# K, V, dK and dV moved in pairs of batches, woT and wqT for two heads per DMA, in a two-block attention backward

## The chip, the cores and the metric

The kernel runs on one core of a Trainium2 chip. The metric is the device time of one execution in microseconds. Before the change it is 1734.54 us, the median of three runs (1733.31 to 1735.66).

## The reference

Two independent attention blocks, A and B, have the same shapes: x is 8 batches x 96 queries x 640, there are 32 heads of width 128, and each head has a cache of 512 keys and values for each batch. All tensors are bf16. For one block the forward pass is

```
q = split_heads(x @ wq)                          # 8 x 32 x 96 x 128
p = softmax(q @ k_cache^T * 128**-0.5)           # 8 x 32 x 96 x 512
o = p @ v_cache
out = merge_heads(o) @ wo                        # 8 x 96 x 640
```

The outputs of A and B stand side by side in the last axis. The kernel returns this output and, for a given grad_out, the gradients of x, k_cache, v_cache, wq and wo of both blocks. With dO = g @ wo^T for a head, these are dV = P^T dO, dP = dO V^T, dS = P * (dP - rowsum(O * dO)), dK = dS^T Q, dQ = dS K, and then dwo = O^T g, dwq = x^T dQ, dx = sum over heads of dQ wq^T.

## The kernel before

One unit of work is a pair of a head and a batch: 2 blocks x 32 heads x 8 batches = 512 units. A head has 96 queries in each batch, so S, P, dP and dS of a unit are 96 x 512 tiles.

**The order is written out by hand in ticks.** Each step is put on a list with a tick and a slot in the tick, `em.add(tick, slot, step)`, and the list is sorted and emitted. A unit starts a new tick: head h begins at `c0t = tick0 + 8*h`, and its batch b at `ct = c0t + b`. `OFF` says how many ticks later each step of the unit is emitted. The framework then orders the instructions of each engine by this emission order and by which are ready in its own model of time; the softmax steps carry a higher priority. Each engine and each DMA queue then runs its list in order. Transposing DMAs and a few others are held in program order (`keep_in_program_order`).

The steps of a unit, with their offset in ticks:

- `c_ld` (0): loads K and V of one batch, 128 KB each, from the queue of SP (L252, L253). Eleven buffers for K, eight for V.
- `c_s1` (2): eight TensorE transposes of K and V into a bank of PSUM (L262, L264), one VectorE copy to `KVT` (L266).
- `c_s2a`, `c_s2b` (3): S = Q K^T (L278), row maximum on VectorE (L280), exp on ScalarE (L290).
- `c_s3a`, `c_s3b` (3): reciprocal (L300), P on GpSimd (L309). P has five buffers.
- `c_s45` (4 and 5): transposes of P (L334), copied to `PT_sb` by ScalarE (L340, three buffers); one tick later O^T = V^T P^T (L325).
- `c_s5b` (5): O * dO on GpSimd (L363).
- `c_s4` (6): dV with natural dO (queries on the partitions) as operand (L351), ScalarE copy to `dV_sb` (L353, six buffers), store from SP (L354).
- `c_s6` (6): dP (L373), row sums (L375), dS on VectorE (L377, three buffers).
- `c_s7` (7): dK with natural Q as operand (L417), ScalarE copy to `dK_sb` (L419, five buffers), store from SP (L420). `c_s78`: transposes of dS (L400), VectorE copy to `dST_sb` (L402, three buffers), and one tick later dQ^T (L391), evacuated at L406.

The steps of a head lie between them, at ticks that `HK` gives against the head's own c0t:

- `pA` (-6) loads a slice of wq (GpSimd's queue). `pV` (-5) loads wo of the head transposed, by a transposing DMA on SP (L180, one buffer). `pB` (-4) allocates Q^T (`QT_h`) and dO^T (`dOT_h`), two buffers each, and lets GpSimd zero the 32 padding columns of `QT_h` where the DMA will transpose it (L191).
- `pC` (which=0 at -3 and -2, which=1 at 0 and 1) makes Q^T from wq and x^T, and dO^T from woT and g^T (L218).
- `pD` (2 and 7 for dO, 3 and 6 for Q) makes the natural form by TensorE transposes (L235) and a VectorE copy. `pN` makes it by one transposing DMA on SP (L245). `BYDMA` chooses: Q goes by DMA from the ninth head of block A on, dO never.
- `pW` (6) loads wq of the head transposed (L197), which only the sum for dx needs.
- `qA` (12 and 16) transposes O and dQ by DMA (L429), `qB` (18, 19) makes dwo (L443), `qD` (20, 23) makes dwq (L463).
- `gU` sums out and dx over groups of eight heads (four in the first and last group of dx) in twelve pieces spread over 26 ticks (L497); the last group's pieces are added on VectorE (L504) and stored (L505).

The first head of block A is early: its woT is emitted at tick +1, behind the loads of the second unit, and its dO^T at +3 and +4.

Of the kernel before, what the change touches and what calls it, by code (L numbers as in the profile page):

```python
# [45 lines left out]
HK = dict(pA=-6, pB=-4, pV=-5, pW=6, pC0=[-3, -2], pC1=[0, 1], pD1=[2, 7], pD0=[3, 6], pN=[-1, 1], qA0=12, qA1=16, qB=[18, 19], qD=[(20, 0, 3), (23, 3, 5)])  # L46
# [6 lines left out]
def build_block(tc, em, tick0, blk, x, kc, vc, wq, wo, g_all, out_all, dx, dk, dv, dwq, dwo, ident, ones, pools, HG=8, first=True):  # L53
# [10 lines left out]
    assert H % HG == 0 and HG % 2 == 0  # L64
# [21 lines left out]
    S = {}  # L86
    G = {}
# [89 lines left out]
    def pV(h):  # L177
        def f():
            woT_h = hd.tile([128, DC, 128], BF16, name="woT_h", bufs=1)
            tc.keep_in_program_order(nc.sync.dma_start_transpose(woT_h[:], wo[h * 128:(h + 1) * 128, :]))  # L180
            HS[(blk, h)]["woT_h"] = woT_h
        return f

    def pB(h):
        def f():
            st = HS[(blk, h)]
            st["QT_h"] = hd.tile([128, B, 128], BF16, name="QT_h")
            st["dOT_h"] = hd.tile([128, B, 128], BF16, name="dOT_h")
            for k in range(2):
                if BYDMA[k](h):  # L190
                    nc.gpsimd.memset(st["dOT_h" if k else "QT_h"][:, :, Sq:128], 0.0)  # L191
        return f

    def pW(h):
        def f():
            wqT_h = hst.tile([128, 1, D], BF16, name="wqT_h")
            tc.keep_in_program_order(nc.sync.dma_start_transpose(wqT_h[:], wq[:, h * 128:(h + 1) * 128]))  # L197
            HS[(blk, h)]["wqT_h"] = wqT_h[:, 0]
        return f

    def pC(h, which, si):
        def f():
# [3 lines left out]
            if which == 0:  # L206
                dst = st["QT_h"][:, b0:b0 + w // Sq, 0:Sq]
                lhs = lambda c: st["wq_h"][:, c, :]
                rhsT = S["xT"]
                sc = scale  # L210
            else:
                dst = st["dOT_h"][:, b0:b0 + w // Sq, 0:Sq]
                lhs = lambda c: st["woT_h"][:, c, :]
                rhsT = S["gT"]
                sc = None
# [6 lines left out]
    BYDMA = [lambda h: not first or h >= 8, lambda h: False]  # L222

    def pD(h, which, half):
        def f():
            st = HS[(blk, h)]
            src = st["dOT_h" if which else "QT_h"]
            name = "dOnat_h" if which else "Qnat_h"
            if half == 0:
                st[name] = hd.tile([128, B, 128], BF16, name=name)  # L230
# [3 lines left out]
            for i in range(nb):  # L234
                nc.tensor.transpose(n_ps[:, i * 128:(i + 1) * 128], src[:, b0 + i, 0:Sq], ident[:])  # L235
            evac("dve", st[name][0:Sq, b0:b0 + nb, :].rearrange("p b d -> p (b d)"), n_ps[:, 0:nb * 128])
        return f

    def pN(h, which):
        def f():  # L240
            st = HS[(blk, h)]
            src = st["dOT_h" if which else "QT_h"]
            name = "dOnat_h" if which else "Qnat_h"
            st[name] = hd.tile([128, B, 128], BF16, name=name)
            tc.keep_in_program_order(nc.sync.dma_start_transpose(st[name][:], src[:].rearrange("p b q -> p (b q)")))  # L245
        return f

    def c_ld(h, b):
        def f():
            K_sb = kvp.tile([128, KC, 128], BF16, name="K_sb", bufs=11)  # L250
            V_sb = kvp.tile([128, KC, 128], BF16, name="V_sb", bufs=8)
            nc.sync.dma_start(K_sb[:], kc[b, h].rearrange("(p c) d -> p c d", c=KC))  # L252
            nc.sync.dma_start(V_sb[:], vc[b, h].rearrange("(p c) d -> p c d", c=KC))  # L253
            CS[(blk, h, b)] = dict(K_sb=K_sb, V_sb=V_sb)
        return f

# [14 lines left out]
    def c_s2a(h, b):  # L271
        def f():
            with tc.high_priority(PRIO_OFF):
# [4 lines left out]
                nc.tensor.matmul(S_ps[:], hs["QT_h"][:, b, 0:Sq], st["KT"], start=True, stop=True)  # L278
# [25 lines left out]
    def c_s3b(h, b):  # L304
        def f():
            with tc.high_priority(PRIO_OFF):
                st = CS[(blk, h, b)]
                P_sb = wk.tile([Sq, Sk], BF16, name="P_sb", bufs=5)
# [4 lines left out]
    def c_s45(k5, k4, k6):  # L313
        def f():
# [23 lines left out]
            if k4 is not None:  # L338
                PT_sb = wk.tile([128, KC * Sq], BF16, name="PT_sb", bufs=3)
# [4 lines left out]
    def c_s4(h, b):  # L344
        def f():
# [4 lines left out]
            for c in range(KC):  # L350
                nc.tensor.matmul(dV_ps[:, c * 128:(c + 1) * 128], P_sb[:, c * 128:(c + 1) * 128], hs["dOnat_h"][0:Sq, b, :], start=True, stop=True)  # L351
            dV_sb = wk.tile([128, KC * 128], BF16, name="dV_sb", bufs=6)
            nc.scalar.activation(dV_sb[:], dV_ps[:], ACT.Identity, scale=1.0)  # L353
            nc.sync.dma_start(dv[b, h].rearrange("(p c) d -> p (c d)", c=KC), dV_sb[:])  # L354
        return f

    def c_s5b(h, b):
        def f():
# [4 lines left out]
            nc.gpsimd.tensor_tensor(prod[:], hs["OT_h"][:, tok], hs["dOT_h"][:, b, 0:Sq], op=ALU.mult)  # L363
# [3 lines left out]
    def c_s6(h, b):  # L367
        def f():
# [4 lines left out]
            nc.tensor.matmul(dP_ps[:], hs["dOT_h"][:, b, 0:Sq], st["VT"], start=True, stop=True)  # L373
            dl_ps = bank([Sq, 1], F32, "dl_ps")
            nc.tensor.matmul(dl_ps[:], st["prod"][:], ones[:, 0:1], start=True, stop=True)  # L375
            dS_sb = wk.tile([Sq, Sk], BF16, name="dS_sb", bufs=3)
# [4 lines left out]
    def c_s78(k8, k7):  # L381
        def f():
# [12 lines left out]
            if k7 is not None:  # L395
# [5 lines left out]
                dST_sb = wk.tile([128, KC * Sq], BF16, name="dST_sb", bufs=3)  # L401
# [8 lines left out]
    def c_s7(h, b):  # L410
        def f():
# [4 lines left out]
            for c in range(KC):  # L416
                nc.tensor.matmul(dK_ps[:, c * 128:(c + 1) * 128], dS_sb[:, c * 128:(c + 1) * 128], hs["Qnat_h"][0:Sq, b, :], start=True, stop=True)  # L417
            dK_sb = wk.tile([128, KC * 128], BF16, name="dK_sb", bufs=5)
            nc.scalar.activation(dK_sb[:], dK_ps[:], ACT.Identity, scale=1.0)  # L419
# [261 lines left out]
```

## Time and profile before

| | |
|---|---|
| median of three runs | 1734.54 us |
| profiled execution | 1731.99 us |
| its span, first to last instruction | 1730.2 us |
| TensorE busy (matmul) | 1720.4 us, 24127 matmuls |
| TensorE weight loads | 1445.2 us |
| VectorE busy | 1415.1 us |
| ScalarE busy | 1475.7 us |
| GpSimd busy | 761.0 us |
| mean granted TensorE clock | 0.999 |
| DMA, HBM read and written | 161.09 MB and 159.12 MB |
| SP's DMA queue, packets | 548208, 80.7% of 16 engines' span |

PE is TensorE's matmul stream, PEld its weight loads, DVE VectorE, ACT ScalarE, POOL GpSimd. SPq and POOLq are the sequencers that issue DMAs. In a waits row stand the engine and line that waited, what ended the wait, the total in us, the number of times and the longest. In a timeline row stand the start and the duration in us, the engine, the line, the tiles written and read, the sizes, the number of instructions merged, and in brackets the idle time of the engine before them with what ended it.

### The profile page before, as it was taken

Reading aid. Unit: us, or ns where it says so; the run is one execution under the profiler, and the core shown is the slowest. Engines: PE = TensorE matmul, PEld = TensorE weight load, DVE = VectorE, ACT = ScalarE, POOL = GpSimd, SP = SyncE. Lnnn points to the kernel's source line nnn. Section 1 sums busy time; section 2 is a strip of 40 time slices with the busy share of each in tenths; the row PEclk is TensorE's granted clock in tenths of the full one; section 3 lists DMA queues with packets and bytes.
Section 4 is the critical chain, followed back from the end, with each engine's and each line's share of the span. In section 5 each row is a group of like instructions: output and inputs, shape, how many; then the busy total and the mean of one; then the engine's idle time right before and its main releaser. Section 6 shows DMA issues by size and latency. Waiting matters only on the chain.

```text
span 1730.2 us, 65292 instructions
## 1 busy us (share of the span) xinstructions
PE 1720.4 (99%) x24127; PEld 1445.2 (84%) x24127; DVE 1415.1 (82%) x2962; ACT 1475.7 (85%) x4081; POOL 761.0 (44%) x1379
## 2 busy tenths in 40 slices
PE   8999999999999999999999999999999999999998
PEld 6888888888888888888888888888888888888886
DVE  7988877888888888888888887788888888888884
ACT  6999988988888888897877999888888888888883
POOL 3444434444344443445455444344443444444441
PEclk9999999999999999999999999999999999999999
DMA  7998998999889999889999998899898999979994
GB/s 214 227 231 225 230 218 213 231 222 215 228 215 226 223 228 218 210 224 259 232 244 240 234 230 229 222 217 232 225 229 220 215 230 237 219 206 215 235 222 120
DMA packets 564946, 385.40 MB, mean 223 GB/s; under 512 B 286145, under 2 KB 553281, under 8 KB 564625
## 3 DMA queue, kind: packets, MB, share of 16 engines
q1 hardware_dynamic: 548208, 333.52, 80.7%
q0 software_dynamic: 16416, 47.70, 10.8%
q8 instruction: 189, 3.10, 0.8%
q14 instruction: 133, 1.08, 0.2%
HBM read 161.09 MB, written 159.12 MB: 185 GB/s over the span
## 4 chain that ended last, share of the span: by engine, by line
PE 97%; DMA 1%; DVE 1%; ACT 0%; POOL 0%; issue 0%; SPq 0%; DVEq 0%; ACTq 0%; POOLq 0%
PE q_ps L218 12%; PE o_ps L497 11%; PE dV_ps L351 7%; PE dK_ps L417 7%; PE kvT_ps L264 6%; PE kvT_ps L262 6%; PE dP_ps L373 6%; PE S_ps L278 6%; PE dwq_ps L463 6%; PE dwo_ps L443 6%; PE dq_dst_ps L400 5%; PE optp_ps L334 5%; PE optp_ps L325 5%; PE dq_dst_ps L391 5%; PE n_ps L235 2%; DMA out_dram<-ob 0%
## 5 line engine op out<-in xcount | busy, mean ns | idle before, releaser
L309 POOL TENSOR_SCALAR P_sb<-E_sb,rinv 96x512 bf16<-96x512 bf16 x512 | 352.2, 688 | 649.0 <-DVE rinv L300 358.8
L377 DVE SCALAR_TENSOR_TENSOR dS_sb<-dP_ps,dl_ps,P_sb 96x512 bf16<-96x512 f32 x512 | 384.7, 751 | 100.4 <-PE dl_ps L375 86.3
L290 ACT ACTIVATE E_sb<-S_ps,negm 96x512 bf16<-96x512 f32 x512 | 348.7, 681 | 122.9 <-DVE negm L280 121.2
L280 DVE TENSOR_REDUCE negm<-S_ps 96x1 f32<-96x512 f32 x512 | 348.1, 680 | 61.4 <-PE S_ps L278 61.2
L266 DVE COPY KVT<-kvT_ps 128x1024 bf16<-128x1024 bf16 x512 | 349.4, 682 | 35.8 <-PE kvT_ps L264 20.0
L419 ACT ACTIVATE dK_sb<-dK_ps 128x512 bf16<-128x512 f32 x512 | 301.7, 589 | 52.0 <-PE dK_ps L417 47.5
L353 ACT ACTIVATE dV_sb<-dV_ps 128x512 bf16<-128x512 f32 x512 | 315.9, 617 | 0.0
L340 ACT ACTIVATE PT_sb<-optp_ps 128x384 bf16<-128x384 bf16 x512 | 254.6, 497 | 1.4 <-PE optp_ps L334 1.4
L363 POOL TENSOR_TENSOR prod<-OT_h,dOT_h 128x96 bf16<-128x96 bf16 x512 | 186.8, 365 | 90.9 <-ACT OT_h L337 82.3
L262 PE MATMUL kvT_ps<-ident,K_sb 128*128 128x128 bf16 x2048 | 197.9, 219 | 0.6 <-DMA K_sb<-in_A_k_cache_dram 0.6
L264 PE MATMUL kvT_ps<-ident,V_sb 128*128 128x128 bf16 x2048 | 197.9, 219 | 0.0
L351 PE MATMUL dV_ps<-dOnat_h,P_sb 96*128 96x128 bf16 x2048 | 197.9, 219 | 0.0
L417 PE MATMUL dK_ps<-Qnat_h,dS_sb 96*128 96x128 bf16 x2048 | 197.9, 219 | 0.0
L373 PE MATMUL dP_ps<-KVT,dOT_h 128*96 128x512 bf16 x512 | 195.1, 381 | 0.0
L278 PE MATMUL S_ps<-KVT,QT_h 128*96 128x512 bf16 x512 | 193.8, 378 | 0.3 <-DVE KVT L266 0.2
L262 PEld LDWEIGHTS <-K_sb 128*128 128x128 bf16 x2048 | 152.9, 98 | 39.0 <-DMA K_sb<-in_A_k_cache_dram 0.8
L402 DVE COPY dST_sb<-dq_dst_ps 128x384 bf16<-128x384 bf16 x512 | 179.0, 350 | 2.2 <-PE dq_dst_ps L400 1.4
L400 PE MATMUL dq_dst_ps<-ident,dS_sb 96*128 96x96 bf16 x2048 | 172.1, 206 | 1.0 <-DVE dS_sb L377 1.0
L334 PE MATMUL optp_ps<-ident,P_sb 96*128 96x96 bf16 x2048 | 171.6, 205 | 0.9 <-POOL P_sb L309 0.9
L325 PE MATMUL optp_ps<-PT_sb,V_sb 128*128 128x96 bf16 x2048 | 172.1, 206 | 0.0
L391 PE MATMUL dq_dst_ps<-dST_sb,K_sb 128*128 128x96 bf16 x2048 | 170.7, 206 | 0.0
L463 PE MATMUL dwq_ps<-dQnat,x_nat 128*128 128x128 bf16 x1920 | 142.8, 219 | 0.0
(76 smaller groups left out, 3492.0 us busy)
## 6 DMA issues: line engine op xcount, KB each, us to landing
out_dram<-dV_sb SPq DMA_DIRECT2D x512, 128.0 KB, 3.3
out_dram<-dK_sb SPq DMA_DIRECT2D x512, 128.0 KB, 3.3
K_sb<-in_A_k_cache_dram SPq DMA_DIRECT2D x256, 128.0 KB, 3.5
V_sb<-in_A_v_cache_dram SPq DMA_DIRECT2D x256, 128.0 KB, 3.4
K_sb<-in_B_k_cache_dram SPq DMA_DIRECT2D x256, 128.0 KB, 3.4
V_sb<-in_B_v_cache_dram SPq DMA_DIRECT2D x256, 128.0 KB, 3.3
out_dram<-dwo_sb POOLq DMA_DIRECT2D x64, 160.0 KB, 3.7
out_dram<-dwq_sb POOLq DMA_DIRECT2D x64, 160.0 KB, 4.8
```

The source lines that it names most:

```text
L262: nc.tensor.transpose(kvT_ps[:, c * 128:(c + 1) * 128], st["K_sb"][:, c, :], ident[:])
L264: nc.tensor.transpose(kvT_ps[:, Sk + c * 128:Sk + (c + 1) * 128], st["V_sb"][:, c, :], ident[:])
L266: nc.vector.tensor_copy(KVT[:], kvT_ps[:])
L280: nc.vector.tensor_reduce(negm[:], S_ps[:], axis=AX.X, op=ALU.max, negate=True)
L290: nc.scalar.activation(E_sb[:], st["S_ps"][:], ACT.Exp, bias=st["negm"][:], scale=1.0, accum_out=rowsum[:])
L309: nc.gpsimd.tensor_scalar(P_sb[:], st["E_sb"][:], st["rinv"][:], 0.0, op0=ALU.mult, op1=ALU.add)
L351: nc.tensor.matmul(dV_ps[:, c * 128:(c + 1) * 128], P_sb[:, c * 128:(c + 1) * 128], hs["dOnat_h"][0:Sq, b, :], start=True, stop=True)
L353: nc.scalar.activation(dV_sb[:], dV_ps[:], ACT.Identity, scale=1.0)
L373: nc.tensor.matmul(dP_ps[:], hs["dOT_h"][:, b, 0:Sq], st["VT"], start=True, stop=True)
L377: nc.vector.scalar_tensor_tensor(dS_sb[:], dP_ps[:], dl_ps[:, 0:1], st["P_sb"][:], op0=ALU.subtract, op1=ALU.mult)
L417: nc.tensor.matmul(dK_ps[:, c * 128:(c + 1) * 128], dS_sb[:, c * 128:(c + 1) * 128], hs["Qnat_h"][0:Sq, b, :], start=True, stop=True)
L419: nc.scalar.activation(dK_sb[:], dK_ps[:], ACT.Identity, scale=1.0)
```

## The change

- `c_ld` runs for even batches only and loads K of two batches in one DMA of 256 KB, and V likewise. Buffers: six pairs for K (before, eleven single ones), four pairs for V (before, eight single ones).
- `pair_out` collects dV, and dK, of two batches in one tile; ScalarE still copies each batch by itself, and the store of 256 KB is issued behind the odd batch. Three pairs of buffers for each (before, six and five single ones).
- `pV` and `pW` run for even heads only, and one transposing DMA brings two heads. woT keeps one buffer, now of two heads; wqT has six pairs (before, twelve single ones).
- Q^T and dO^T of a head become one tile `QD_h`, and natural Q and natural dO one tile `QDnat_h`, each with two buffers. `NBYDMA` keeps the choice of before: Q by DMA from the ninth head on, dO by TensorE.
- P has four buffers (before five); PT, dS and dST two (before three).
- Ticks: pV -5 to -6, pW 6 to 2, pC1 0, 1 to -1, 0, pN for Q -1 to 0, the transpose of dQ 16 to 15, dwo 18, 19 to 17, 18, dwq (20: three columns blocks, 23: two) to (19: two, 20: three). The first head's woT stays at +1, with the second head's in the same DMA, which before came at tick -3 of the second head.

```diff
-HK = dict(pA=-6, pB=-4, pV=-5, pW=6, pC0=[-3, -2], pC1=[0, 1], pD1=[2, 7], pD0=[3, 6], pN=[-1, 1], qA0=12, qA1=16, qB=[18, 19], qD=[(20, 0, 3), (23, 3, 5)])
+HK = dict(pA=-6, pB=-4, pV=-6, pW=2, pC0=[-3, -2], pC1=[-1, 0], pD1=[2, 7], pD0=[3, 6], pN=0, qA0=12, qA1=15, qB=[17, 18], qD=[(19, 0, 2), (20, 2, 5)])
...
     def pV(h):
         def f():
-            woT_h = hd.tile([128, DC, 128], BF16, name="woT_h", bufs=1)
-            tc.keep_in_program_order(nc.sync.dma_start_transpose(woT_h[:], wo[h * 128:(h + 1) * 128, :]))
-            HS[(blk, h)]["woT_h"] = woT_h
+            woT = hd.tile([128, DC, 256], BF16, name="woT", bufs=1)
+            tc.keep_in_program_order(nc.sync.dma_start_transpose(woT[:], wo[h * 128:(h + 2) * 128, :]))
+            for k in range(2):
+                WT[h + k] = woT[:, :, k * 128:(k + 1) * 128]
...
     def pB(h):
         def f():
-            st["QT_h"] = hd.tile([128, B, 128], BF16, name="QT_h")
-            st["dOT_h"] = hd.tile([128, B, 128], BF16, name="dOT_h")
-            for k in range(2):
-                if BYDMA[k](h):
-                    nc.gpsimd.memset(st["dOT_h" if k else "QT_h"][:, :, Sq:128], 0.0)
+            QD = hd.tile([128, 2, B, 128], BF16, name="QD_h")
+            HS[(blk, h)]["QD_h"] = QD
+            n = NBYDMA(h)
+            if n:
+                nc.gpsimd.memset(QD[:, 0:n, :, Sq:128], 0.0)
...
+            wqT = hst.tile([128, 2, D], BF16, name="wqT", bufs=6)
+            tc.keep_in_program_order(nc.sync.dma_start_transpose(wqT[:], wq[:, h * 128:(h + 2) * 128]))
...
-    BYDMA = [lambda h: not first or h >= 8, lambda h: False]
+    def NBYDMA(h):
+        return 1 if not first or h >= 8 else 0
...
     def c_ld(h, b):
         def f():
-            K_sb = kvp.tile([128, KC, 128], BF16, name="K_sb", bufs=11)
-            V_sb = kvp.tile([128, KC, 128], BF16, name="V_sb", bufs=8)
-            nc.sync.dma_start(K_sb[:], kc[b, h].rearrange("(p c) d -> p c d", c=KC))
-            nc.sync.dma_start(V_sb[:], vc[b, h].rearrange("(p c) d -> p c d", c=KC))
-            CS[(blk, h, b)] = dict(K_sb=K_sb, V_sb=V_sb)
+            K2 = kvp.tile([128, 2, KC, 128], BF16, name="K_sb", bufs=6)
+            V2 = kvp.tile([128, 2, KC, 128], BF16, name="V_sb", bufs=4)
+            for (t_, src) in ((K2, kc), (V2, vc)):
+                nc.sync.dma_start(t_[:].rearrange("p b c d -> p b (c d)"),
+                                  src[b:b + 2, h].rearrange("b (p c) d -> p b (c d)", c=KC))
+            for k in range(2):
+                CS[(blk, h, b + k)] = dict(K_sb=K2[:, k], V_sb=V2[:, k])
...
+    def pair_out(name, dram, h, b, src_ps):
+        if b % 2 == 0:
+            S[name] = wk.tile([128, 2, KC * 128], BF16, name=name, bufs=3)
+        t_ = S[name]
+        nc.scalar.activation(t_[:, b % 2, :], src_ps, ACT.Identity, scale=1.0)
+        if b % 2 == 1:
+            nc.sync.dma_start(dram[b - 1:b + 1, h].rearrange("b (p c) d -> p b (c d)", c=KC), t_[:])
...
-                P_sb = wk.tile([Sq, Sk], BF16, name="P_sb", bufs=5)
+                P_sb = wk.tile([Sq, Sk], BF16, name="P_sb", bufs=4)
...
-                PT_sb = wk.tile([128, KC * Sq], BF16, name="PT_sb", bufs=3)
+                PT_sb = wk.tile([128, KC * Sq], BF16, name="PT_sb", bufs=2)
...
-            dV_sb = wk.tile([128, KC * 128], BF16, name="dV_sb", bufs=6)
-            nc.scalar.activation(dV_sb[:], dV_ps[:], ACT.Identity, scale=1.0)
-            nc.sync.dma_start(dv[b, h].rearrange("(p c) d -> p (c d)", c=KC), dV_sb[:])
+            pair_out("dV_sb", dv, h, b, dV_ps[:])
...
-            dS_sb = wk.tile([Sq, Sk], BF16, name="dS_sb", bufs=3)
+            dS_sb = wk.tile([Sq, Sk], BF16, name="dS_sb", bufs=2)
...
-                dST_sb = wk.tile([128, KC * Sq], BF16, name="dST_sb", bufs=3)
+                dST_sb = wk.tile([128, KC * Sq], BF16, name="dST_sb", bufs=2)
...
         early = first and h == 0
-        em.add(c0t + (1 if early else -3 if first and h == 1 else HK["pV"]), SL_SETUP + 1 if early else SL_HEAD, pV(h))
-        for k in range(2):
-            if BYDMA[k](h):
-                em.add(c0t + HK["pN"][k], SL_HEAD + 0.5, pN(h, k))
-        em.add(c0t + HK["pW"], SL_HEAD, pW(h))
+        if h % 2 == 0:
+            em.add(c0t + (1 if early else HK["pV"]), SL_SETUP + 1 if early else SL_HEAD, pV(h))
+            em.add(c0t + HK["pW"], SL_HEAD, pW(h))
+        if NBYDMA(h):
+            em.add(c0t + HK["pN"], SL_HEAD + 0.5, pN(h))
...
         for b in range(B):
             ct = c0t + b
-            em.add(ct + OFF["ld"], SLOTS["LOAD"], c_ld(h, b))
+            if b % 2 == 0:
+                em.add(ct + OFF["ld"], SLOTS["LOAD"], c_ld(h, b))
```

## The prediction

> **What bounds the kernel now.** I read the page first, then the waits, a stretch of the timeline in mid-kernel, and the timelines of the first and last microseconds. From the page:
>
> ```profile
> span 1730.2 us, 65292 instructions
> PE 1720.4 (99%) x24127; PEld 1445.2 (84%) x24127; DVE 1415.1 (82%) x2962; ACT 1475.7 (85%) x4081; POOL 761.0 (44%) x1379
> DMA  7998998999889999889999998899898999979994
> PE 97%; DMA 1%; DVE 1%; ACT 0%; POOL 0%; issue 0%; SPq 0%; DVEq 0%; ACTq 0%; POOLq 0%
> ```
>
> TensorE works through all but 9.8 us of the span, and the chain that ended last is TensorE's for 97% of it; but the DMA engines are busy too, at about nine tenths. So the waits of TensorE decide, of which these are the largest:
>
> ```profile
> PE warm_ps L601 <- DVE warm L598: 1.6, 1, 1.6
> ...
> PE dq_dst_ps L400 <- DVE dS_sb L377: 1.0, 2, 0.7
> PE optp_ps L334 <- POOL P_sb L309: 0.9, 3, 0.6
> ...
> PE q_ps L218 <- DVE gT L123: 0.6, 1, 0.6
> PE kvT_ps L262 <- DMA K_sb<-in_A_k_cache_dram: 0.6, 1, 0.6
> ...
> PE q_ps L218 <- DMA woT_h<-in_A_wo_dram: 0.2, 1, 0.2
> ```
>
> It waited for a DMA twice, 0.8 us in all. A matmul's duration overlaps the next one's, so a full busy row could hide gaps; the timeline settles that:
>
> ```profile
> 1004.07 0.39 PE L351 MATMUL dV_ps<-dOnat_h,P_sb 96*128 96x128 bf16 x4
> 1004.29 0.38 PE L373 MATMUL dP_ps<-KVT,dOT_h 128*96 128x512 bf16 x1
> 1004.48 0.69 POOL L309 TENSOR_SCALAR P_sb<-E_sb,rinv 96x512 bf16<-96x512 bf16 x1 [1.85 <-PE dV_ps L351]
> 1004.51 0.16 PE L375 MATMUL dl_ps<-ones,prod 128*96 128x1 bf16 x1
> ```
>
> Four matmuls of 128 columns start within 0.22 us, and the one of 512 columns gives way after 0.22 us. By the starts in the trace a matmul takes the array for 56 ns (128 columns), 43 (96), 163 (384), 136 (320), 216 (512) and 26 (one column). With the counts of the groups that is 10808 x 56 + 8192 x 43 + 1280 x 163 + 2304 x 136 + 1024 x 216 + 512 x 26 ns = 1,714 us. Only some 16 us of the span is not matmuls back to back: 1.6 us before the first, about 5 us of waits in the first 40 us and 1.3 us near the end, about 4 us behind the last matmul, and rounding. The kernel is bound by the number of its matmul columns.
>
> The Trainium skill (Perfetto Trace Analysis, Identifying the Most-Contended Engine) says that matmul busy time is no measure of how near a kernel is to its roofline, and that the share of weight loads is a better one. By it the 84% of the weight-load row would leave room, and the next bound would be the DMA engines (the fourth rival, priced from rows below); the starts in the trace do not bear that out here, and the weight loads lie under matmuls that are longer than they are.
>
> **The change part by part.** The profiled execution took 1731.99 us: span 1730.2, and 1.8 around it. The median is 2.55 us above it.
>
> *Matmuls.* None is added or removed. The last clause of the change is already true before: natural dO's 512 transposes (L235) stay, natural Q's 64 of the first eight heads too, and 56 transposing DMAs make the rest. TensorE's 1,714 us stand: 0.
>
> *Fewer DMAs.* SP issues 1,024 plain DMAs less (a K load holds its sequencer for 0.44 us, V 0.40, a store 0.38: about 420 us), and 64 transposing ones less at 1.25 us (80 us, or nothing if one for two heads takes twice as long). SP is only a queue: past the start no matmul waited for what it issues. Bytes and the 1 KB and 256-byte packets stay. Bounds on the total: 0, and a gain of 10 us if the DMA engines were the bound (of the trace's 43,248 packets of 4 bytes, which close each DMA, 1,024 x 16 go, at 10 ns over 16 engines). I take 0, since TensorE doesn't wait there.
>
> *When K and V come.* For even batches the K slot frees as before (the ninth tick of the unit eleven back), the V slot one tick later (it now waits for the odd unit of the pair seven back). A tick is 3.32 us, the mean distance of two S matmuls. In the trace V is issued a median of 4.0 us after its old slot was free, and landed a median of 7.6 us before its first transpose, after the first thirty units never under 1.76 us. Delaying each even V to its new slot moves 93 of 252, and none comes too late, even with 0.9 us more for the larger transfer (128 KB takes 3.4 to 3.5 us to land, x_nat with 320 KB 3.6). Bounds: 0, and 8.7 us if every even V came 4.2 us later (the shortfalls summed after the thirtieth unit). I take 0. The wait stands on SP, and the next stores and loads queue behind it; half of SP's work is gone.
>
> *Paired stores.* ScalarE's copies stay as they are (0.62 and 0.59 us x512). The store waits for the odd copy; three pairs give a slot back four ticks after it is filled, against 3.3 us to land. 0.
>
> *Smaller buffers.* P is written at 1004.48, and the dS that reads its new slot's old content (one tick back) ended at 1002.64: 1.8 us spare. PT, dS and dST have one tick between last read and next write. 0.
>
> *One tile for Q^T and dO^T.* This adds a wait. GpSimd zeroes the padding of a head's tile at tick -4 (0.31 us, x56); the slot is now free only when dP of the head two before has run for its last batch, at tick -3. Before, it waited for S alone:
>
> ```profile
> POOL QT_h L191 <- PE S_ps L278: 8.9, 22, 0.4
> ```
>
> Behind the memset in GpSimd's queue stands P of tick -3, for which TensorE's transposes (L334) wait one tick later. In the stretch above dP ends at 1004.67 and P starts at 1004.48; a memset at 1004.7 would push P to about 1005.05, by 0.57 us. P was ready 0.99 us or more ahead of its transpose after the thirtieth unit (median 2.18). The first writes of Q^T come after dP in TensorE's own order. Bounds: 0, and 56 x 0.31 = 17.4 us if none of the memset found cover. I take 0, by the slack that was never under 0.99.
>
> *Moved ticks.* dO^T one tick earlier still writes behind dP of the old tile. woT has five ticks to land as before (3.8 to 4.0 us). wqT is asked for two ticks after its slot is free. Natural Q lands 4.9 us after its issue, with seven ticks to go. dwo and dwq move by one to three ticks, and tick 3 of a head becomes the lightest (1,536 columns of head work instead of 1,920, 0.16 us shorter); the tightest margin there, KVT before S (L278), was at least 0.37. 0, at worst 64 x 0.16 = 10 us.
>
> *The start.* Here one matmul of the chain waits for woT:
>
> ```profile
> 10.69 0.40 PE L262 MATMUL kvT_ps<-ident,K_sb 128*128 128x128 bf16 x4 [0.59 <-DMA K_sb<-in_A_k_cache_dram]
> 11.73 0.99 PE L218 MATMUL q_ps<-gT,woT_h 128*128 128x384 bf16 x5 [0.20 <-DMA woT_h<-in_A_wo_dram]
> ```
>
> The same bytes as before stand ahead of woT (x, wq, two K and V, g), and it landed at 11.68 us, 0.59 behind the second V at 11.09. For two heads I estimate twice that, so a landing at 12.3: +0.6. The 0.59 us wait for the second K goes, but g lands some 0.9 us later; both disappear in the wait for woT. Bounds: -3.7 us (all waits of the first 40 us gone) and +5.2 (woT took 5.2 us from issue to landing; a second one behind it whole). I take +0.6, from the landings, because the queue was moving bytes all the time.
>
> TensorE's clock in the start: weight loads of the warm-up stand 0.43 us apart, later matmuls of that size 0.22, and the profile grants 0.999 over the span. The Trainium skill (TensorE: Matmul & The Clock Gate, Part 1) says that an idle window of about 3.4 us halves the clock again. By it the +5.2 would become about +7; at +0.6 nothing changes.
>
> *The end.*
>
> ```profile
> 1704.34 1.95 SPq L429 DMA_TRANSPOSE dQnat<-dQT_h  x1
> 1709.00 1.17 PE L463 MATMUL dwq_ps<-dQnat,x_nat 128*128 128x128 bf16 x18
> 1727.14 0.49 DVE L504 TENSOR_TENSOR ob<-o_ps,dx_acc 128x320 bf16<-128x320 f32 x1 [0.78 <-DMA out_dram<-ob]
> ```
>
> The last dQ lands at 1708.10, 4.8 us after the start of the matmuls that make it (1703.27); its use moves one tick up, to about 4.5 us after: +0.3. The drain behind the last matmul (three ob buffers) stays. Bounds 0 and +1.3.
>
> Sum: 1730.2 + 0.6 + 0.3 = 1731.1 span, 1732.9 profiled, **1735.4 us** as median. A measurement of this kernel can tell about 0.2% (3.5 us) from no change.
>
> **The rivals.**
>
> - *The padding decides* (slower). If P is held more than 0.99 us behind dP in the tick of the memset, TensorE stands before L334 in 56 heads. At 0.31 us each: 1752. For it: dP comes late in its tick and P starts at the same time. Against: the margin. From 0.06 us a head on it is past 0.2%.
> - *K or V late* (slower). 8.7 us, and 6.4 more in the first thirty units, if every even V lands 4.2 us later: 1744 to 1750. For it: the V slot. Against: no V would have been late by the trace.
> - *woT of two heads late at the start* (slower). 5.2 instead of 0.6: 1740.
> - *The DMA engines are the bound* (faster). Nine tenths busy speaks for it, and 10 us less gives 1724.5; that TensorE waited 0.8 us for DMAs speaks against it.
> - *The start's waits go* (faster): K's second load comes with the first. -3.7 us: 1731. g behind the larger loads speaks against it.
>
> **How the numbers follow.** Forecast (no change in mid-kernel, +0.9 at the ends) 0.62, its own range 1732.5 to 1738; padding 0.11, K or V 0.09, woT 0.08; DMA engines 0.05, start 0.05. Slower by over 0.2%: 0.28; within: 0.62; faster: 0.10. The range leaves out the DMA case (0.05) and the upper end of the padding and K cases (some 0.12): 1731 to 1746.
>
> **What would show it.** PE at 24127 matmuls and about 1,721 us busy; no PE wait on K, V or P past 40 us; a wait of GpSimd's memset for dP of up to a tick, x56, with no PE wait on P beside it; SP's issues halved and not longer each; woT landing near 12.3 us with some 0.8 to 1 us of PE wait. The prediction is wrong if TensorE's waits past the start sum to over 3 us, or if the ends move by over 3 us.

## The result, and the profile after

| | before | after |
|---|---|---|
| median | 1734.32 us (1733.31 to 1735.66, four runs) | 1744.69 us (1740.59 to 1746.70, four runs) |
| ratio after / before, 95% interval | | 1.0056 [1.0035, 1.0077] |
| profiled execution, its span | 1731.99, 1730.2 us | 1746.70, 1744.9 us |
| mean granted TensorE clock | 0.999 | 0.997 |
| GpSimd's and SP's DMA packets | 16416 and 548208 | 16416 and 529776 |

The changed kernel is 0.56% slower. The time lies inside the range of the prediction, but the forecast itself, no change, is wrong. The changed kernel's executions also differ from each other by much more than those of the kernel before, which matters below, where the number of executions over 1737 us is given beside each median. One execution of the kernel before, 2513 us at a granted clock of 0.654, is in none of the counts.

From the page of the changed kernel, the lines that answer to the first fence of the prediction:

```profile
span 1744.9 us, 62607 instructions
PE 1725.8 (99%) x24127; PEld 1448.9 (83%) x24127; DVE 1421.5 (81%) x2962; ACT 1472.0 (84%) x4081; POOL 758.2 (43%) x1379
DMA  8899888998999987899898999889988999988983
PE 1%; DMA 1%; DVE 1%; issue 0%; POOL 0%; DVEq 0%
```

The work of each engine is the same within 7 us, and the matmuls are the same 24127. The span is 14.7 us longer and TensorE's busy time 5.4 us. The chain row, 97% TensorE before, follows only the drain at the end this time and says nothing of the rest. The waits of TensorE over 0.2 us show two rows of more than 1 us that were not there before, the first two:

```profile
PE dV_ps L365 <- ACT dwq_sb L160: 4.4, 1, 4.4
PE dl_ps L387 <- DVE ob L514: 3.1, 1, 3.1
PE warm_ps L612 <- DVE warm L609: 1.6, 1, 1.6
PE dq_dst_ps L412 <- DVE dS_sb L389: 1.0, 2, 0.7
PE optp_ps L348 <- POOL P_sb L323: 1.0, 3, 0.6
PE q_ps L221 <- DMA woT<-in_A_wo_dram: 0.9, 1, 0.9
PE q_ps L221 <- DVE gT L125: 0.6, 1, 0.6
PE tp_ps L124 <- DMA x_nat<-in_A_x_dram: 0.4, 1, 0.4
PE kvT_ps L278 <- DMA V_sb<-in_A_v_cache_dram: 0.3, 1, 0.3
```

**Where the 14.7 us lie.** In both traces I took from the distance between the starts of two matmuls the time that the first one's columns need (56 ns for 128 columns, and so on as in the prediction) and summed what is left by windows of 107.5 us. From the second window to the seventh, and from the tenth to the fifteenth, both kernels lose 1.1 to 1.3 us in each window: mid-kernel is unchanged. (This base depends on how the times per matmul are rounded, and is next to nothing with the rounded ones of the prediction; only the differences between the kernels are read.) The start (first window) goes from 8.3 to 9.5, the window from 752 us from 1.1 to 8.4, the one from 860 us from 1.1 to 6.0, the last full one from 2.9 to 3.3. That is 13.8 us, and the stretch behind the last matmul's start grew from 4.5 to 5.4 us. So 12 of the 14.7 us lie in two places of one stand each, both at the turn from block A to block B, where the last head groups of A, the loads of x and g of B (`ld_tmp`, `g_nat`, `x_nat`) and the first transposes of B's woT meet.

The first stand, in the timeline of the changed kernel:

```profile
819.31 0.60 POOL L457 DMA_DIRECT2D out_dram<-dwo_sb  x1 [0.95 <-ACT dwo_sb L160]
822.07 0.83 PE L473 MATMUL dwq_ps<-dQnat,x_nat 128*128 128x128 bf16 x12
829.02 0.38 ACT L160 ACTIVATE dwq_sb<-dwq_ps 128x256 bf16<-128x256 f32 x1 [5.38 <-DMA out_dram<-dwo_sb]
829.46 0.58 PE L365 MATMUL dV_ps<-QDnat_h,P_sb 96*128 96x128 bf16 x4 [4.42 <-ACT dwq_sb L160]
830.33 2.08 PE L473 MATMUL dwq_ps<-dQnat,x_nat 128*128 128x128 bf16 x18
```

ScalarE's copy of dwq needs one of the six `row640` buffers, which `ld_tmp`, `dwo_sb` and `dwq_sb` share. That buffer still holds a dwo whose store was issued at 819.31 and landed only at 828.92, after 9.6 us; the median of this store is 4.1 us. ScalarE works in order, dV's bank waits behind the copy, and TensorE stands 4.6 us (by the starts of the matmuls; the rows above count from the end of the matmul before and have 0.2 us less). Then it runs at half rate: the eighteen dwq matmuls of the last line start 107 ns apart instead of 56, and the granted clock is 0.50 until 835.3, which costs another 2.8 us.

The second stand, in the same timeline:

```profile
881.50 2.60 SPq L182 DMA_TRANSPOSE woT<-in_B_wo_dram  x1
882.52 0.89 POOL L134 DMA_DIRECT2D g_nat<-in_grad_out_dram  x1 [0.50 <-PE o_ps L507]
885.71 0.54 POOL L515 DMA_DIRECT2D out_dram<-ob  x1
887.79 0.58 POOL L515 DMA_DIRECT2D out_dram<-ob  x1 [1.14 <-DVE ob L514]
888.97 11.17 SPq L439 DMA_TRANSPOSE Onat<-OT_h  x1
898.70 0.49 DVE L514 TENSOR_TENSOR ob<-o_ps,dx_acc 128x320 bf16<-128x320 f32 x1 [4.08 <-DMA out_dram<-ob]
899.24 0.16 PE L387 MATMUL dl_ps<-ones,prod 128*96 128x1 bf16 x1 [3.14 <-DVE ob L514]
```

VectorE's `ob` waits for one of three buffers, whose stores take 11 to 13 us here; TensorE stands 3.3 us and loses 1.6 more at half rate. What was issued beside them is as late: woT landed 14.9 us after its issue, g_nat 13.8 (before 7.9), and the issue of the transpose of O held SP for 11.2 us (1.25 when nothing is in its way).

Busy time by stretch of the changed kernel; the columns are the stretch, its length, the five engines' busy times (with instructions), TensorE's granted clock, the busy share of the DMA engines (packets overlap, so it can be over 1) and the GB/s that they moved:

```profile
600.00:640.00 40.00, 40.00 (x583) 34.23 (x581) 33.31 (x71) 34.68 (x96) 17.52 (x32) 1.00 0.94 221
...
824.00:836.00 12.00, 7.58 (x74) 6.07 (x72) 3.86 (x9) 3.16 (x9) 2.57 (x5) 0.72 1.00 195
...
884.00:892.00 8.00, 8.00 (x130) 7.17 (x127) 6.19 (x15) 6.01 (x19) 4.71 (x9) 1.00 1.25 79
```

The last of these stretches in the kernel before:

```profile
884.00:892.00 8.00, 8.00 (x108) 6.65 (x107) 6.33 (x14) 6.46 (x19) 4.37 (x8) 1.00 1.13 304
```

From 884 to 892 us the DMA engines are busy all the time by this count, and they move 79 GB/s instead of the 221 of mid-kernel and the 304 of the kernel before. The packets of 256 bytes, which are those of the transposing DMAs, are about as many (1241, before 1187) but take 101 ns each on average, against 26 ns before: 1241 x 101 ns over 16 engines and 8 us is 0.98 of the share of 1.25. So transfers become slow at the second stand, and what waits for a transfer stands. Around the first stand the fall is smaller, 195 GB/s from 824 to 836 us; landings are late there too (9 to 12 us for what was issued from 819 to 825 us).

### The profile page after: what moved, and what is told of

Its sections match the earlier page's. It is cut to its first block, busy times and chain, and to the rows that moved or that the text cites. A ratio compares the mean times of both kernels' runs of the same rounds, so it can differ in the third digit from the quotient of the medians.

```text
span 1744.9 us, 62607 instructions
## 1 busy us (share of the span) xinstructions
PE 1725.8 (99%) x24127; PEld 1448.9 (83%) x24127; DVE 1421.5 (81%) x2962; ACT 1472.0 (84%) x4081; POOL 758.2 (43%) x1379
## 3 DMA queue, kind: packets, MB, share of 16 engines
q1 hardware_dynamic: 529776, 333.45, 79.6%
q0 software_dynamic: 16416, 47.70, 9.4%
## 5 line engine op out<-in xcount | busy, mean ns | idle before, releaser
L375 POOL TENSOR_TENSOR prod<-OT_h,QD_h 128x96 bf16<-128x96 bf16 x512 | 187.5, 366 | 83.6 <-ACT OT_h L351 75.3
L365 PE MATMUL dV_ps<-QDnat_h,P_sb 96*128 96x128 bf16 x2048 | 198.1, 219 | 4.4 <-ACT dwq_sb L160 4.4
L429 PE MATMUL dK_ps<-QDnat_h,dS_sb 96*128 96x128 bf16 x2048 | 197.9, 219 | 0.0
L385 PE MATMUL dP_ps<-KVT,QD_h 128*96 128x512 bf16 x512 | 195.4, 382 | 0.0
L292 PE MATMUL S_ps<-KVT,QD_h 128*96 128x512 bf16 x512 | 194.2, 379 | 0.4
L418 ACT ACTIVATE dQT_h<-dq_dst_ps 128x96 bf16<-128x96 f32 x512 | 128.2, 250 | 25.3 <-DVE dST_sb L414 5.6
```

The source lines that it names most:

```text
L385: nc.tensor.matmul(dP_ps[:], hs["QD_h"][:, 1, b, 0:Sq], st["VT"], start=True, stop=True)
```

## The experiments

Two theories had to be told apart, and the runs undo one part of the change, or make one part alone.

- *Buffers*: the shared buffers `row640` and `ob` are too few in the new order; the moved ticks put a taker right behind a store.
- *Transfers*: the larger DMAs (woT for two heads, K, V, dK, dV for two batches) make the transfers at the turn slow, and any buffer there will do to make TensorE stand.

In the expectations of the first runs, T is the first theory, with the moved ticks as its cause, W the second with woT's DMA and P the second with those of K, V, dK and dV.

### Ticks of dQ, dwo and dwq put back

```diff
-HK = dict(... qA0=12, qA1=15, qB=[17, 18], qD=[(19, 0, 2), (20, 2, 5)])
+HK = dict(... qA0=12, qA1=16, qB=[18, 19], qD=[(20, 0, 3), (23, 3, 5)])
```

> The kernel after, with the ticks of the transpose of dQ, of dwo and of dwq as before (16; 18, 19; 20 and 23). In the kernel after, TensorE stands for 4.6 and 3.3 us at the turn from block A to block B, each time with the DMA queues jammed (stores of dwo and ob from GpSimd's queue took 9.6 and 11 to 13 us to land) and runs at half rate for some 5 and 4 us behind it. Theory T (the moved ticks put the dwq copy's shared 640-column buffer behind a dwo store that has not landed): the first stand of 4.6 us and its half rate go, about 7 us less: 1737; the second may stay. Theory W (the transposing DMA of two heads of woT jams the queues): both stands remain, 1742 to 1747. Theory P (the 256 KB loads and stores jam them): as W.

Measured: 1746.64 us (1746.41 to 1746.83, four runs), ratio 1.0080 [1.0065, 1.0095]. There is no stand at the turn any more (1.6 and 1.5 us lost in the two windows), but 0.4 to 1.3 us more are lost in nearly every window of the kernel: among others P comes late for TensorE, ten waits of 2.1 us together against three of 1.0. So the time is what W and P expected and their reason is not: both had the two stands stay. T had the first stand go, which it did, and the time fall, which it did not. All the pairs are in this kernel, and yet its transfers keep 227 to 293 GB/s at the second turn (876 to 900 us), and its four executions agree within 0.5 us. One thing differs in the order there: woT is issued 4.2 us ahead of g_nat, and lands after 4.7 us; in the changed kernel it is 1.0 us ahead and lands after 14.9.

### The same ticks alone, in the kernel before

```diff
-HK = dict(... qA0=12, qA1=16, qB=[18, 19], qD=[(20, 0, 3), (23, 3, 5)])
+HK = dict(... qA0=12, qA1=15, qB=[17, 18], qD=[(19, 0, 2), (20, 2, 5)])
```

> The kernel before, with only the ticks of the transpose of dQ, of dwo and of dwq moved as in the change. Theory T: a stand of 3 us or more at the turn of the blocks, with ScalarE's dwq copy waiting for a dwo store: 1738 to 1742. Theories W and P: no stand, 1732 to 1736.

Measured: 1742.27 us (1741.85 to 1742.48, four runs), ratio 1.0055 [1.0040, 1.0070]. Again nothing at the turn, and some 0.5 us more per window all along, so neither expectation holds: the time is at the upper end of T's, but without T's stand. In these two runs half of the moves, whichever half it is, makes small waits all through the kernel.

### All moved ticks, in the kernel before

```diff
-HK = dict(pA=-6, pB=-4, pV=-5, pW=6, pC0=[-3, -2], pC1=[0, 1], pD1=[2, 7], pD0=[3, 6], pN=[-1, 1], qA0=12, qA1=16, qB=[18, 19], qD=[(20, 0, 3), (23, 3, 5)])
+HK = dict(pA=-6, pB=-4, pV=-6, pW=2, pC0=[-3, -2], pC1=[-1, 0], pD1=[2, 7], pD0=[3, 6], pN=[0, 1], qA0=12, qA1=15, qB=[17, 18], qD=[(19, 0, 2), (20, 2, 5)])
```

> The kernel before with every moved tick of the change (pV, pW, pC1, pN, the transpose of dQ, dwo, dwq) and nothing else: single loads and stores, buffers as before. Theory 'ticks and pairs together' (the ticks put the dwq copy right behind a dwo store for the same buffer, and the pairs make that store land late): a wait at L160 of at most 1 us, 1733 to 1736. Rival 'ticks' (the order alone makes the waits at the turn): 1740 or more, with the wait for the dwo store over 3 us. The tick moves of dwo and dwq alone gave 1742.3 by small waits all along; if those stay here too, 1742 without a wait at the turn.

Measured: 1733.67 us (1732.33 to 1739.29, eleven runs), ratio 1.0002 [0.9991, 1.0013]. Taken together the moved ticks cost nothing, in mid-kernel too (1.1 to 1.3 us lost per window). The rival that the order alone makes the stands falls; *ticks and pairs together* had expected this time. The profiled execution had one short stand at the turn, 1.9 us before L375 at 887.6 us, beside landings of 12 us.

### One head per woT DMA

```diff
-            woT = hd.tile([128, DC, 256], BF16, name="woT", bufs=1)
-            tc.keep_in_program_order(nc.sync.dma_start_transpose(woT[:], wo[h * 128:(h + 2) * 128, :]))
+            woT = hd.tile([128, DC, 128], BF16, name="woT", bufs=1)
+            tc.keep_in_program_order(nc.sync.dma_start_transpose(woT[:], wo[h * 128:(h + 1) * 128, :]))
...
```

> The kernel after, with woT loaded for one head per DMA, as before. Theory W: the jam at the turn of the blocks is shorter, both stands go, and the start loses its extra 1.1 us: 1732 to 1736, with woT landing in under 9 us at the turn. Theory T: the first stand stays, 1740 to 1745. Theory P: as T.

Measured: 1738.58 us (1732.91 to 1746.71, ten runs, seven of them over 1737), ratio 1.0038 [1.0019, 1.0057]. The profiled execution was a good one: span 1732.8, with one stand of 0.6 us before dV. The median lies between what W and what T and P expected, and the executions reach into both. So the loss is no fixed price of this kernel: it comes in some executions and not in others, and where those over 1737 us lose it was not seen.

### K, V, dK and dV one batch per DMA

```diff
-            K2 = kvp.tile([128, 2, KC, 128], BF16, name="K_sb", bufs=6)
-            V2 = kvp.tile([128, 2, KC, 128], BF16, name="V_sb", bufs=4)
+            K_sb = kvp.tile([128, KC, 128], BF16, name="K_sb", bufs=11)
+            V_sb = kvp.tile([128, KC, 128], BF16, name="V_sb", bufs=8)
...
-            S[name] = wk.tile([128, 2, KC * 128], BF16, name=name, bufs=3)
+        t_ = wk.tile([128, KC * 128], BF16, name=name, bufs=6 if name == "dV_sb" else 5)
...
```

> The kernel after, with K, V, dK and dV moved one batch per DMA and with their buffers of before. Theory P: no jam, no stands, 1733 to 1737. Theories T and W: the stands stay, 1740 to 1747.

Measured: 1735.16 us (1733.55 to 1740.20, seven runs, three over 1737), ratio 1.0021 [1.0008, 1.0034]. In the profiled execution, the fastest, the wait for the dwo store is 1.2 us and TensorE's stand 0.4. The median is what P expected; the three over 1737 us are not.

### More buffers at the two stands

One more `row640` and two more `ob` take the room of the third pair of dV. First both, then each by itself:

```diff
-        return hd.tile([128, D], BF16, name=name, tag="row640", bufs=6)
+        return hd.tile([128, D], BF16, name=name, tag="row640", bufs=7)
...
-                ob = wk.tile([128, w], BF16, name="ob", bufs=3)
+                ob = wk.tile([128, w], BF16, name="ob", bufs=5)
...
-            S[name] = wk.tile([128, 2, KC * 128], BF16, name=name, bufs=3)
+            S[name] = wk.tile([128, 2, KC * 128], BF16, name=name, bufs=2 if name == "dV_sb" else 3)
```

> The changed kernel with two more buffers where TensorE's two long waits at the turn of the blocks came from: row640 seven instead of six, ob five instead of three; the room comes from the pairs of dV, two instead of three. Theory 'buffers' (the wait is ScalarE's dwq copy for a row640 buffer whose dwo store has not landed, and VectorE's ob for its stores): both waits go, with the half rate behind them, 1744.7 - 4.6 - 2.6 - 3.3 - 1.5 = 1732.7, so 1732 to 1737, and no row of a ScalarE wait at L160 for out_dram<-dwo_sb over 1 us. Rival 'transfers' (the transposing DMAs of two heads and the large loads hold up the queues, and whatever waits for a transfer next takes the place): the wait moves to another line, 1740 or more. Rival 'dV' (two pairs of dV come free too late): waits for out_dram<-dV_sb on ScalarE, 1746 or more.

Measured: 1741.14 us (1740.32 to 1742.09, five runs), ratio 1.0043 [1.0030, 1.0056]. Both old stands are gone, and TensorE stands 6.5 us at 891.3 us instead, for a dV store that took 18.1 us to land (3.2 in the median). The rows of the waits:

```profile
ACT dV_sb L267 <- DMA out_dram<-dV_sb: 8.1, 1, 8.1
PE dK_ps L429 <- ACT dV_sb L267: 6.4, 1, 6.4
```

This wait is partly made by the experiment, which took a pair from dV; those shown for the next kernel are not.

> The same with row640 at seven and ob left at three. Theory 'buffers': the dV wait of 4.6 us and its half rate go, the ob wait stays: 1744.7 - 7.2 = 1737.5 (1734 to 1740). Rival 'transfers': 1741 or more.

Measured: 1741.50 us (1738.27 to 1744.98, five runs), ratio 1.0045 [1.0033, 1.0057]. The wait of the dwq copy is gone; the store's wait falls on `ld_tmp` now, and TensorE stands 1.9 us for a late load of it at 835 us and 2.7 us for `ob` at 891 us:

```profile
POOL ld_tmp L100 <- DMA out_dram<-dwo_sb: 5.5, 1, 5.5
PE dl_ps L387 <- DVE ob L514: 2.6, 1, 2.6
PE tp_ps L112 <- DMA ld_tmp<-in_grad_out_dram: 1.7, 1, 1.7
```

> The same with ob at five and row640 left at six. Theory 'buffers': the ob wait of 3.3 us and its half rate go, the wait for the dwo store stays: 1744.7 - 4.8 = 1739.9 (1737 to 1742). If the first wait alone makes the second (by the delay and the slower clock), nothing is won: 1744.

Measured: 1745.23 us (1733.56 to 1747.82, six runs, five of them from 1743.85 on), ratio 1.0058 [1.0036, 1.0079]. The profiled execution was the one of 1733.56 us. It is a kernel with all the transfers in pairs, and it shows what the others lack: in the same stretch, with the same DMAs in the same order, the engines moved 293 GB/s, woT landed in 8.3 us and g_nat in 7.5. Its table of stretches:

```profile
876.00:884.00 8.00, 8.00 (x118) 6.94 (x116) 6.02 (x14) 6.24 (x17) 4.68 (x8) 1.00 1.02 294
880.00:888.00 8.00, 8.00 (x110) 6.71 (x109) 5.98 (x13) 6.41 (x18) 5.17 (x10) 1.00 1.10 293
884.00:892.00 8.00, 8.00 (x101) 6.35 (x98) 6.30 (x13) 5.88 (x17) 6.22 (x10) 1.00 1.11 290
```

What follows from the three: where TensorE stands is set by the buffers, and that it stands by how fast the transfers run. The theory *buffers* falls as the cause: it expected 1732 to 1737 of the first of them, 1734 to 1740 of the second and 1737 to 1742 of the third.

### The large loads in three pieces

```diff
-        em.add(tick0 + B + OFF["s5"] - 2, SL_LOAD, setup_nat(1))
-        em.add(tick0 + B + OFF["s8"] - 2, SL_LOAD, setup_nat(0))
+        for t in range(0, TT, 2):
+            em.add(tick0 + B + OFF["s5"] - 2 + t // 2, SL_LOAD, setup_nat(1, t, 2))
+            em.add(tick0 + B + OFF["s8"] - 2 + t // 2, SL_LOAD, setup_nat(0, t, 2))
```

> The changed kernel with block B's natural g and x (0.98 MB each, two DMAs on GpSimd's queue) in three DMAs each, one tick apart. Theory 'transfers' (at the turn the two-head woT transpose and the large loads run in the DMA engines at once, everything issued beside them lands 10 to 18 us late, and TensorE stands at whatever waits for one): the second jam (874 to 900 us) goes, no landing there over 8 us, the first (818 to 833) stays: 1744.7 - 4.8 = 1740, at best 1737. Rival 'transpose' (the woT transpose alone makes the jam, with or without the loads): landings of 10 us and more stay, 1743 or more.

Measured: 1740.27 us (1736.43 to 1745.82, eight runs), ratio 1.0042 [1.0028, 1.0056]. The time is what *transfers* expected, but not for its reason: in the profiled execution the second turn still has landings of 11 to 16 us and 133 GB/s from 880 to 888 us, and the stand there happens to be short (0.8 us). The first stand stays, as expected (3.6 us). The pieces were issued only 1.4 and 2.0 us apart, so they hardly spread the load; whether a wider spread would help was not tried.

> Both: natural g and x in three DMAs each, row640 at seven, ob at five, dV in two pairs. In the run with these buffers and the large loads whole, TensorE stood 6.5 us at 891 us for a dV store; the wait for the dwo store was gone. Theory 'transfers': with the loads spread too, no wait over 1 us at either turn: 1732 to 1736. Rival 'transpose': 1739 or more, with a wait of over 2 us between 885 and 905 us.

Measured: 1739.74 us (1737.30 to 1742.50, six runs), ratio 1.0032 [1.0021, 1.0044], with a stand of 3.9 us for a dV store at 900.5 us. Cutting the large loads into three doesn't keep the transfers from getting slow, as the rival had expected.

> The kernel before with natural g and x spread in the same way. Theory 'transfers': before has the same jam, shorter, and its buffers cover it in most executions: no change of the median, 1732 to 1734, and no execution over 1737. If the median falls by over 2 us, the jam had a price before too.

Measured: 1733.22 us (1732.14 to 1738.99, eleven runs, three over 1737), ratio 1.0005 [0.9994, 1.0016]. No change of the median, as expected; that no execution would be over 1737 was wrong, so this cut is no cure in the kernel before either.

### woT, K, V, dK and dV all single

The edits of the two kernels with woT alone and with K, V, dK and dV alone, put together.

> The changed kernel with woT, K, V, dK and dV single again: of the change only the moved ticks, the shared tiles of Q and dO, the wqT pairs and the smaller buffers of P, PT, dS and dST are left. Theory 'pairs' (the larger DMAs of woT and of K, V, dK, dV make the jam at the turn worse, nothing else of the change costs anything): 1732.5 to 1734.5, the time of the kernel before. Rival 'buffers and tiles' (a part of the rest has a price of its own): 1736 or more.

Measured: 1732.66 us (1732.11 to 1734.87, eleven runs, none over 1737), ratio 0.9995 [0.9986, 1.0004]. With these five transfers single, the rest of the change costs nothing. The stretches of its profiled execution:

```profile
868.00:876.00 8.00, 8.00 (x111) 6.71 (x109) 6.28 (x16) 6.03 (x18) 4.15 (x7) 1.00 0.99 239
876.00:884.00 8.00, 8.00 (x129) 7.17 (x127) 6.33 (x15) 6.19 (x17) 5.06 (x9) 1.00 1.09 239
884.00:892.00 8.00, 8.00 (x103) 6.36 (x101) 6.30 (x14) 6.39 (x20) 6.18 (x11) 1.00 1.09 291
892.00:900.00 8.00, 8.00 (x99) 6.35 (x98) 6.89 (x15) 5.95 (x17) 3.61 (x8) 1.00 0.93 275
```

No stretch falls under 239 GB/s. Its median is the lowest of all, but by an amount that can't be told from the kernel before, so no version here beats it.

**Together.** Sorted by which transfers are in pairs, with the executions over 1737 us:

| transfers in pairs | kernels | executions over 1737 us |
|---|---|---|
| none of the five | all single | 0 of 11 |
| none of the five | before | 5 of 71 |
| none of the five | before with all ticks; before with spread loads | 2 of 11; 3 of 11 |
| woT alone | K, V, dK, dV single | 3 of 7 |
| K, V, dK, dV alone | woT single | 7 of 10 |
| all | after and its five variants with other buffers or loads | 32 of 34 |

The two runs with half of the moved ticks are left out: their loss is another one, spread over the whole kernel. wqT is in pairs in every version of the changed kernel, also in the one with the five single, where it costs nothing. In the series of the two kernels with one kind of pair, the kernel before had none of its 16 executions over 1737 us.

What is shown: with the five transfers single the rest of the change (all moved ticks, shared tiles, smaller buffers of P, PT, dS and dST) costs nothing, with them in pairs nearly every execution is over 1737 us, and with each of the two kinds of pair alone a part of them is. The moved ticks alone cost nothing either, but the pairs are not shown to be enough without them: with the ticks of dQ, dwo and dwq put back, the pairs made no stand at the turn, and the pairs without any moved tick were not run. So what costs time is the pairs in this order. That the loss lies at the turn was seen in the profiled executions of the changed kernel and of four of its variants; of the two kernels with one kind of pair only an execution under 1737 us was profiled.

What stays open: why the DMA engines fall to a third of their rate there. The slow stretch of the changed kernel begins behind the two-head woT transpose, and most of its busy time is that of 256-byte packets; but with the same DMAs in the same order an execution ran at 293 GB/s, so the sequence makes the slow stretch likely and doesn't force it. Whether it is the size of the K, V, dK and dV transfers that counts or that a pair's buffer comes free as a whole, the loads or the stores, the transposes at the turn or those elsewhere, was not separated.

## Why the prediction was right or wrong

That the time fell into the range is luck. The forecast was 1735.4, and the range reached up to 1746 for parts of the cases of the padding, of late K or V and of a woT 5.2 us late; none of these happened, and no rival had a loss at the turn.

- *Matmuls*: right. 24127 matmuls, and mid-kernel loses the same in every window as before.
- *Fewer DMAs*: this is the step that failed. It put the cost between 0 and a gain of 10 us, "since TensorE doesn't wait there"; the runs put 12 us of loss at the turn in the profiled execution. The reason given was true of the trace of before and no bound: it said that transfers were early enough at their size, not that they would stay so in pairs. The rival on the DMA engines had the right resource (nine tenths busy) and the wrong sign: it asked only what fewer closing packets would give back.
- *Paired stores*: "3.3 us to land" is a median over the kernel. The paired dV store did land in 3.2 us in the median, but the row that matters is the slowest stretch: up to 16.3 us for a dV store (18.1 with more buffers elsewhere) and 9.6 to 13 us for the stores on GpSimd's queue, which the change didn't even touch. The prediction named no buffer behind a store on that queue (`ob` only for the drain at the end); `row640` and `ob` are such, and they were where TensorE stood.
- *When K and V come*: right. Past the first thirty units K landed at least 5.7 us before its first transpose and V 3.5 us, medians 12.9 and 9.8, more than before. TensorE waited for neither past the start.
- *One tile for Q^T and dO^T*, and the rival of the padding: the price of 0 was right, but the added wait did not come. GpSimd zeroed the padding 0.59 us or more behind the end of that dP in all 56 heads and stood idle before it for 0.02 us in all; it ran behind `prod` nearly always, with P already done. P's waits stayed at three and 1.0 us. The smallest margin of P, the last head aside (there the kernel before has 0.06 already, which the prediction's 0.99 leaves out), shrank from 0.99 to 0.39 us, which looks like the 0.57 of this step and isn't: the kernel before with all the moved ticks and no shared tile has the same 0.39, at the same unit. The version with all five transfers single, which keeps the shared tile, costs nothing.
- *Smaller buffers*: right by the same version.
- *Moved ticks*: 0 was right for all of them together (1733.67). Half of the moves costs about the 10 us given as the worst in the kernel before (1742.27 against 1732.82) and more inside the changed kernel (1746.64, 13.8 over the kernel before).
- *The start*: +1.2 instead of +0.6 us. woT landed at 12.8 us (forecast 12.3), with 0.9 us of wait (forecast 0.8 to 1), the second K's wait went, as said; but x_nat came late by 0.4 and V by 0.3. With woT single the start still loses 9.2 us, with K and V single 8.7, with both 8.4 against 8.3 before: the larger K and V ahead cost more than woT itself, which the estimate from woT's landing left out.
- *The end*: +0.4 us before the last matmul (forecast +0.3), and 0.9 more behind it, where the drain was said to stay.
- *What would show it wrong*, waits of TensorE past the start of over 3 us together, is what happened: 7.5 us in two rows.

The half rate belongs to the size. In the seven profiled executions with a stand of 0.7 us or more at the turn, every stand of 3.3 us or more (3.3, 3.6, 3.9, 4.6, 6.5) was followed by matmuls at half their pace, at a granted clock of 0.50, which cost 1.5 to 2.8 us more, and none of 2.7 us or less (2.7, 1.9, 1.9, 1.2 and shorter) was. The length alone does not fix the moment: at the first stand of the changed kernel the clock fell at 828.5 us, 0.9 us before TensorE went on, at the second at 900.2 us, 0.9 us after it had gone on at full pace. All its changes in that stretch of the trace, at 828.5, 835.3, 900.2 and 903.6 us, lie whole multiples of 3.41 us apart. So these stands don't give a sharp limit: the one of 2.7 us lay across such a time (892.8 us, counted in steps of 3.41 us from the changes of clock in its own trace), and a shorter one than 3.3 us isn't shown to be safe. The Trainium skill (TensorE: Matmul & The Clock Gate, Part 1) gives about 3.4 us of idle time for this; the stand of 3.3 us is a little shorter and was caught. A wait of that length is to be priced with some 2 us on top, as the prediction did for the start and nowhere else.

## What to carry to other kernels

Where the DMA engines are nine tenths busy, joining transfers into larger ones need not be free even if every one of them lands early in the trace: price it at the stretch where the most transfers meet, by the slowest landing there, and list every buffer that is freed by a store on any queue, not only those that the change touches. When TensorE stands at such a place, another buffer may only move the stand, as it did here; look at the GB/s of the stretch beside the busy share, and change what is in flight. And take the spread of the executions as a result: a median that rises with the spread, while good executions keep the old time, points to a collision rather than to added work. Where a margin shrinks by the amount that you predicted, look for it in a run without the part that you hold responsible: here P's was there too.

## What the runs showed of the hardware

- The DMA engines can be busy all the time and move a third of their rate in mid-kernel: 79 GB/s at a share of 1.25 in the changed kernel, 73 at 1.20 (876 to 884 us) in the one with more buffers, with 221 in mid-kernel. In the first of these a fifth of the 256-byte packets take over 220 ns, with a median of 18.
- It is not a fixed effect of a sequence: two executions of nearly the same program had 79 and 290 GB/s between 884 and 892 us.
- The issue of a transposing DMA held SP's queue for 11.2 us in the changed kernel and 12.9 us in the one with more buffers, both issued in the slow stretch with the transposing DMA of woT unfinished. Elsewhere it takes about 1.25 us for one head of O, and 2.4 us in the median for two heads of woT.
- The granted clock of TensorE fell to 0.50 and rose again at times that lie multiples of 3.41 us apart, once 0.9 us after the stand that goes with it was over (900.2 us in the changed kernel).
